# Block 1's fourth pair of heads: three products a chunk, or six DMAs a chunk, in an attention and two-layer MoE kernel

## The chip, the cores and the metric

The kernel runs on one core of a Trainium2 chip. The time is device microseconds of one execution, and less is better. Besides the runs that are timed there is one profiled execution, whose trace is read here.

## The reference

The kernel computes a linear attention with a decaying state and, on its output, two feed-forward layers. Only the state's recurrence and the order of the columns matter here.

```python
# q, k, v, alpha: (4, 8, 768, 48); B, H, S, D
for t in range(S):
    state = alpha[:, :, t, :, None] * state + np.einsum('bhd,bhe->bhde', k[:, :, t], v[:, :, t])
    y[:, :, t] = np.einsum('bhd,bhde->bhe', q[:, :, t], state)
x = y.transpose(0, 2, 1, 3).reshape(B * S, H * D)        # 3072 x 384
x = (x @ w_a) * (x @ w_b) @ w_out                         # d_ff 1536
h = x @ w_in                                              # d_ff 2048
out = (np.maximum(h, 0) + alpha2 * np.minimum(h, 0)) @ w_out2
```

The weights arrive in 64-bit floating point. The kernel converts each on the core to a high and a low 32-bit part, and every large product is made of three (high by high, low by high, high by low).

## The kernel before, in words

**Blocks and chunks.** The 3072 tokens are cut into 24 chunks of 128 (`CH`; one chunk holds 128 time steps of one batch entry), and these into 6 blocks of four chunks (`BC`). Chunk g belongs to block g // 4. Blocks 0 and 1 hold the first 256 steps of all four batch entries. A block's attention output is `x` (`xt[n]`, 128 partitions x high/low x `NJ` = 4 pairs x 512 tokens), and the first layer reads three of the four pairs (`KT` = 3, 384 columns).

**The fourth pair.** The heads have 48 columns and sit in slots of 64 partitions, two to a pair, so four pairs have 16 free partitions in each slot, and the columns of the fourth pair have to fill the free partitions of the first three. That is done in three ways (lines 539 to 677). In block 0 the values are laid out in advance (`vg`) and products place them. In block 1 (`moved`, lines 601 to 617) ScalarE copies the fourth pair's output from PSUM to `shift` (L607), three products with a shifting matrix (L611) add it to the other pairs, and only three pairs are split into high and low (`split_h` L657 on ScalarE, `split_l` L661 on VectorE, two instructions each). In blocks 2 to 5 four pairs are split, and after the block's last chunk six DMAs on SP's queue (L677) copy 16 partitions each from the fourth pair to the others.

**One chunk of attention** (`chunk(g)`, from block 1 on): two scans (L402, L412) and a product with q and k (`mul`, L417) on VectorE; a transpose of k (`kps`, L453) and the scores (`A`, L481) on TensorE; the masked scores (`ev_a`, `As`, L496) on VectorE; `pe_cross` (L558, L581) on TensorE; `mid` (L587) on VectorE; `pe_own` (L558, L565) on TensorE; the next state (`kept`, L632) on VectorE; then the split to `x`. Scores and output of all chunks share one PSUM buffer (`pring`), so a chunk's scores wait until the chunk before has been split.

**The first layer** goes over `SEGMENTS`: block 0 with units 0 and 1, block 1 with units 0 and 1, block 0 with units 2 and 3, and so on; a unit is 256 of the 1536 hidden columns. Each step k of `flat` has nine matmuls `pa`, nine `pb` and, two steps later (`LAG`), nine `acc` (L699, L700, L702). The `pa` and `pb` keep the order of k. Steps 0 to 3 are block 0's with units 0 and 1, step 4 is the first that reads block 1. A unit's weights `wa`, `wb`, `wo` are converted by VectorE and ScalarE (L254 to L283; the last instruction is L283), at most two conversions at a time.

**The order** of every engine's instructions, and of the DMA issues on SP, is fixed at build time by a planner (`Graph.run`). Each operation has an engine, a duration, a latency, a key and what it waits for. The planner steps through its own time and gives an engine that becomes free the ready operation with the lowest key. A user on another engine may begin `HOP` = 250 ns after the end. Where TensorE would be free for over 500 ns, `fill` writes small matmuls that compute nothing (`wp`, L185) for 0.7 of the planned gap, up to block 2. On the chip each engine goes through its fixed order and waits on semaphores.

Of the kernel before, what the change touches and what calls it, by code (L numbers as in the profile page):

```python
# [11 lines left out]
F32 = mybir.dt.float32  # L12
# [9 lines left out]
P = 128  # L22
CH = 128
HC = CH // 2
BC = 4
MB = BC * CH
# [7 lines left out]
ON_PE = (("a", 0), ("b", 0), ("o", 0))  # L34


MM = 228
HOP = 250
T_MOE = 30000
STRETCH = 1.2  # L40
URGENT = 40000
# [8 lines left out]
class Graph:  # L50
# [7 lines left out]
    def add(self, eng, dur, fn, key, deps=(), lat=0, after=(), pool=None):  # L58
        o = Op()
        o.pool, o.hold = pool, []  # L60
        o.eng, o.dur, o.fn, o.key, o.lat = eng, dur, fn, key, lat
        o.users, o.soft, o.ready, o.end, o.need, o.n = [], [], 0, None, 0, len(self.ops)
        for d in {x for x in deps if x is not None}:
            d.users.append(o)
            o.need += 1
        for d in {x for x in after if x is not None}:
            d.soft.append(o)
            o.need += 1
        self.ops.append(o)
        return o  # L70
# [69 lines left out]
def body(tc, akq, v, vg, w_a, w_b, w_o1, w_in, w_o2, beta, out):  # L140
    nc = tc.nc
    NG, H = akq.shape[0], v.shape[2]
    KT, NT = out.shape[1], out.shape[2]
# [3 lines left out]
    NJ = H // 2  # L147
    D = KT * P // H
    GR = 64 - D
    NA = NJ * (CH + 1) + 1  # L150
    NC = NJ * CH
    NB = NG // BC

    with ExitStack() as ctx:
# [3 lines left out]
        xpool, cpool, gpool, tp = pool("xpool", 2), pool("cpool", 2), pool("gpool", 2), pool("tp", 2)  # L158
# [4 lines left out]
        eye = gpool.tile([P, P], F32, name="eye", tag="a_sb")  # L163
# [14 lines left out]
        def fill(t0, t1):  # L178
# [14 lines left out]
            out=mask, in_=mask, pattern=[[1, P]], compare_op=ALU.is_ge, fill=0.0,  # L193
# [2 lines left out]
        nc.scalar.copy(plus, eye)  # L196
        nc.scalar.mul(minus, eye, -1.0)


        shift = gpool.tile([P, KT + 1, P], F32, name="shift", tag="x2")  # L200
        nc.gpsimd.memset(shift, 0.0)
        for t in range(KT):
            for i in range(2):
                nc.gpsimd.tensor_copy(
                    out=shift[:, t, 64 * i + D : 64 * i + 64],
                    in_=eye[:, 64 * i + GR * t : 64 * i + GR * (t + 1)],
                )

        G = Graph(fill)
        units, uses = {}, {}  # L210
# [2 lines left out]
        flat = [(n, i, s) for s, (n, u0, u1) in enumerate(SEGMENTS) for i in range(2 * u0, 2 * u1)]  # L213
        at = [T_MOE + int(k * 27 * MM * STRETCH) for k in range(len(flat) + LAG + 1)]
        due, block_at = {}, {}
# [111 lines left out]
        for u in range(NU1):  # L327
            for nm, src in (("a", w_a), ("b", w_b), ("o", w_o1)):
                x = nm, u
# [16 lines left out]
        st = [dict() for _ in range(NG)]  # L346
        xt, xuse, xdone = {}, {}, {n: [] for n in range(NB)}
        xring, lring, rring, vring, zring = Ring(2), Ring(2), Ring(2), Ring(2), Ring(1)
        aring, pring, kring, sring, yring = Ring(1), Ring(1), Ring(1), Ring(1), Ring(1)
        before = {"scan": None}  # L350
        accfree = [[] for _ in range(KT)]
        state = [[] for _ in range(BC)]
# [1 line left out]
        def chunk(g):  # L354
            s = st[g]
            n, c = divmod(g, BC)
            start, moved, end = n == 0, n == 1, n == NB - 1
            key = block_at[n] - (BC - c) * 9500 - 6000 if n else c * 1000 - 100000
            cols = slice(c * CH, (c + 1) * CH)

            def A(eng, dur, fn, deps, early=0, lat=0, after=()):
                return G.add(eng, dur, fn, key - early, deps, lat, after)
# [3 lines left out]
            if spare is None:  # L366
                rwait, lwait = rring.take(), lring.take()
                rhold, lhold = rring.last(), lring.last()
            else:
                rwait, lwait, rhold, lhold = (), (), [], []  # L370
# [27 lines left out]
            lv = A("SP", 1250 if start else 720, load_v, vring.take(), 12000, 3000)  # L398
# [23 lines left out]
            slack = SLACK if not start else 0  # L422
            k1 = q1 = A("DVE", 1220, mul, [lq, sa], 0, slack)
# [3 lines left out]
            zs = None  # L427
            if not start:
# [5 lines left out]
                zs = A("DVE", 360, decayed, [r, *state[c]])  # L434
# [14 lines left out]
            if not (start and end):  # L449
# [9 lines left out]
                kbank, w, hold = bank(0)  # L459
                x = A("PE", 480, pe_k, [k1, *w])  # L460
# [23 lines left out]
            def ev_a(i):  # L484
                def f():
                    if i == 0:
                        s["At"] = tp.tile([P, 2 * NJ * CH], F32, name="As", tag="As", bufs=1)
                        w = CH if start else HC
                        s["As"] = s["At"][:, 0 : 2 * NJ * w].rearrange("p (i j t) -> p i j t", i=2, j=NJ)
                    if start:  # L490
                        m = mask.rearrange("p (o t) -> p o t", o=1).to_broadcast([P, NJ, CH])
                        nc.vector.tensor_tensor(out=s["As"][:, i], in0=s["A"][i], in1=m, op=ALU.mult)
                        return
                    m = mask[:, 0:HC].rearrange("p (a o t) -> p a o t", a=1, o=1).to_broadcast([P, 2, NJ, HC])
                    a = s["A"].rearrange("p i (j t) -> p i j t", t=HC)
                    nc.vector.tensor_tensor(out=s["As"], in0=a, in1=m, op=ALU.mult)  # L496
                return f

            w = sring.take()
            if start:  # L500
                (b0, w0, h0), (b1, w1, h1) = bank(1), bank(2)
                abanks = (b0, b1)
                pa = A("PE", 1200, pe_a, [k1, q1, *w0, *w1])
                a0 = A("DVE", 660, ev_a(0), [pa, *w])
                a1 = A("DVE", 660, ev_a(1), [pa, a0])
                masked.append(a1)
                h0.append(a0)
                h1.append(a1)
            else:
                pa = A("PE", 600, pe_a, [k1, q1, *pring.take()])  # L510
                a0 = a1 = A("DVE", 700, ev_a(0), [pa, halved[0], *w], 0, slack)
                pring.use(a0)

            def slot_of_head(j, i):
# [2 lines left out]
            def y_of(k, rows=slice(0, P), t=slice(0, CH)):  # L517
                return s["y"][rows, k // 2, k % 2, t]
# [4 lines left out]
            if start:  # L523
# [7 lines left out]
                w = aring.take()  # L531
# [16 lines left out]
                            nc.tensor.matmul(y_of(k, half(p)), s["vg"][:, k, p, :],  # L548
                                             s["As"][:, KT // 2, 2 * (KT % 2) + p, :], start=False, stop=k > 0)

                py = A("PE", 1600, pe_y, [a0, a1, lv, q1, *pring.take()])
                yhold = pring.last()
            else:
                part_of = lambda h: slice(h * HC, (h + 1) * HC)
# [43 lines left out]
                pc = A("PE", 850, pe_cross, [a0, ks, lv, *pring.take()])  # L598
                yhold = pring.last()
                kring.use(pc)  # L600
                z1 = A("DVE", 360, mid, [pc, zs])
                py = A("PE", 850, pe_own, [z1, zs, q1])
                yhold.append(z1)
            if moved:
                def ev_3():
                    s["y3"] = shift[:, KT, :]
                    nc.scalar.copy(s["y3"], y_of(KT))  # L607

                def pe_m():
                    for k in range(KT):  # L610
                        nc.tensor.matmul(y_of(k), shift[:, k, :], s["y3"], start=False, stop=k > 0,  # L611
                                         skip_group_check=True)

                lhold.append(py)
                x = A("ACT", 280, ev_3, [py, *yring.take()])
                py = A("PE", 750, pe_m, [x])
                yring.use(py)
            lhold.extend((pa, py))
            if spare is not None:
                for k, ops in ((spare, rhold), (spare + 1, lhold)):  # L620
# [5 lines left out]
            if not end:  # L626
# [7 lines left out]
                x = A("ACT" if start else "DVE", 360, kept, [ds] if start else [z1, py])  # L634
# [5 lines left out]

            nt = KT if start or moved else NJ
            sring.use(py)
            vring.use(py)

# [16 lines left out]
            if c == 0:  # L663
                xring.take()
                xuse[n] = xring.last()
            s["xh"] = A("ACT", 620, split_h, [py], after=[st[n * BC]["xh"]] if c else ())
            xl = A("DVE", 700, split_l, [s["xh"]])
            yhold.append(xl)
            xdone[n].append(xl)
            if c < BC - 1 or start or moved:  # L670
                return
            moves = []
            for t in range(KT):
                for i in range(2):
                    def move(t=t, i=i):
                        z = xt[n].bitcast(F32)
                        nc.sync.dma_start(z[64 * i + D : 64 * i + 64, :, t, :],  # L677
                                          z[64 * i + GR * t : 64 * i + GR * (t + 1), :, KT, :])

                    moves.append(A("SP", 600, move, xdone[n], 0, 2500))  # L680
            xdone[n] = moves

        masked, halved = [], []
        for g in range(NG):
# [19 lines left out]
        def up(key, deps, x, w, o, after=()):  # L704
# [9 lines left out]

            op = G.add("PE", 9 * MM, f, key, deps, after=after, pool=mpool)
            uses[w].append(op)
# [97 lines left out]
        for k, (n, i, s) in enumerate(flat):  # L814
            u, o = divmod(i, 2)
            x = lambda n=n: xt[n]
            b = {}
            pa, ma, ba = up(at[k], [done["a", u][o], *xdone[n]], x, ("a", u), o,
                            [up_before])
# [30 lines left out]
        for k in range(2 * NU2):  # L850
            b = {}
            key = t0 + k * (t1 - t0) // (2 * NU2)
            _, c = conv((w_in, w_o2)[k % 2][k // 2], f"s{k % 2}", f"s{k % 2}", key,
                        [stored[k - 2]] if k >= 2 else part_users[k], lambda r, b=b: b.update(r=r))
# [10 lines left out]
        for k in range(2 * NU2):  # L865
            x = "id"[k % 2], k // 2
# [54 lines left out]
        for k, (n, i) in enumerate(flat2):  # L921
            if i == 0:
                ld = load_x2(n)
            u, o = divmod(i, 2)
# [97 lines left out]
```

## Time and profile before

| | |
|---|---|
| time, median of 3 runs | 967.0 us (966.63 to 967.01) |
| profiled execution, its own time | 966.85 us |
| span of its instructions | 965.2 us |
| mean granted clock of TensorE | 0.999 |
| busy: PE, VectorE, ScalarE, GpSimd | 952.7, 600.4, 253.9, 4.4 us |

Times in rows count from the first instruction. A timeline row has the start, the duration, the engine, the line, what is written and read, and how many instructions it merges; in brackets stands how long the engine had been idle, and what ended that. Matmuls of a row overlap the next row's, so a step's cost is the distance from its start to the next start.

### The profile page before, as it was taken

The numbers are of one execution on the slowest core, as the hardware profiler recorded it, in microseconds if no ns is written. First come the engines' busy times: TensorE is split into PE (matmuls) and PEld (weight loads), VectorE is DVE, ScalarE is ACT, GpSimd is POOL, SyncE is SP. The second block draws the span as 40 slices with busy tenths as digits, with TensorE's granted clock in tenths as the row PEclk, the third lists the DMA queues.
The fourth block names the chain that finished last, engine by engine and source line by source line (L and its number), as shares of the span: only waits on it lengthen the run. The fifth ranks groups of instructions, "written<-read, shape, count | busy, mean of one in ns | idle before, by whom it ended". The sixth has DMA issues, their size and how long they took to land.

```text
span 965.2 us, 15549 instructions
## 1 busy us (share of the span) xinstructions
PE 952.7 (99%) x6667; PEld 770.4 (80%) x6667; DVE 600.4 (62%) x887; ACT 253.9 (26%) x422; POOL 4.4 (0%) x18
## 2 busy tenths in 40 slices
PE   6999999999999999999999999999999999999998
PEld 5778888778877887887788888888888888888886
DVE  7999888578668868865332254555555545545554
ACT  2444443233333333332221211111111111111111
POOL 1000000000000000000000000000000000000000
PEclk9999999999999999999999999999999999999999
DMA  8971000145456545742065550010100200200000
GB/s 317 407 287 51 12 1 12 45 145 180 150 179 204 206 167 191 240 153 79 25 210 197 196 196 1 27 72 1 65 33 1 89 10 0 99 1 1 33 1 33
DMA packets 31076, 104.09 MB, mean 108 GB/s; under 512 B 3488, under 2 KB 4256, under 8 KB 31008
## 3 DMA queue, kind: packets, MB, share of 16 engines
q1 hardware_dynamic: 30864, 102.97, 30.2%
q8 instruction: 52, 0.85, 0.4%
q10 hardware_dynamic: 144, 0.13, 0.0%
q14 instruction: 16, 0.13, 0.0%
HBM read 74.78 MB, written 26.74 MB: 105 GB/s over the span
## 4 chain that ended last, share of the span: by engine, by line
PE 99%; DVE 0%; DMA 0%; ACT 0%; issue 0%; DVEq 0%; ACTq 0%
PE acc L699 12%; PE acc L702 12%; PE acc L700 12%; PE pi L699 7%; PE pi L702 7%; PE pi L700 7%; PE pb L699 5%; PE pa L699 5%; PE pa L700 5%; PE pb L700 5%; PE pb L702 5%; PE pa L702 5%; PE wp L185 2%; PE y L558 2%; PE kps L453 1%; PE A L481 1%
## 5 line engine op out<-in xcount | busy, mean ns | idle before, releaser
L722 ACT CAST gh<-ng 128x512 fp32r<-128x512 f32 x96 | 59.6, 621 | 328.6 <-DVE ng L935 275.0
L931 DVE TENSOR_SCALAR ng<-pi,betaT 128x512 f32<-128x512 f32 x96 | 72.1, 751 | 106.7 <-PE pi L702 105.8
L726 DVE TENSOR_TENSOR gl<-ng,gh 128x512 fp32r<-128x512 f32 x96 | 66.3, 691 | 79.9 <-ACT gh L722 79.9
L699 PE MATMUL pi<-x,v 128*128 128x512 f32 x288 | 113.3, 393 | 0.0
L700 PE MATMUL acc<-gh,v 128*128 128x512 f32 x288 | 113.1, 393 | 0.0
L702 PE MATMUL acc<-gl,v 128*128 128x512 f32 x288 | 112.9, 392 | 0.0
L700 PE MATMUL pi<-x,v 128*128 128x512 f32 x288 | 112.7, 391 | 0.0
L699 PE MATMUL acc<-gh,v 128*128 128x512 f32 x288 | 112.1, 389 | 0.0
L829 DVE TENSOR_TENSOR a_sb<-a_sb,pb 128x512 f32<-128x512 f32 x72 | 49.4, 686 | 96.5 <-PE pb L702 96.4
L699 PE MATMUL pa<-x,wa 128*128 128x512 f32 x216 | 86.7, 401 | 0.0
L699 PE MATMUL pb<-x,wb 128*128 128x512 f32 x216 | 86.6, 401 | 0.0
L699 PE MATMUL acc<-gh,wo 128*128 128x512 f32 x216 | 86.6, 401 | 0.0
L702 PE MATMUL acc<-gl,wo 128*128 128x512 f32 x216 | 84.9, 393 | 0.0
L700 PE MATMUL pa<-x,wa 128*128 128x512 f32 x216 | 84.7, 392 | 0.0
L700 PE MATMUL pb<-x,wb 128*128 128x512 f32 x216 | 84.6, 392 | 0.0
L700 PE MATMUL acc<-gh,wo 128*128 128x512 f32 x216 | 84.6, 392 | 0.0
L826 ACT COPY a_sb<-pa 128x512 f32<-128x512 f32 x72 | 42.2, 587 | 151.0 <-PE pa L702 151.0
L702 PE MATMUL pi<-x,v 128*128 128x512 f32 x288 | 81.5, 391 | 0.0
L722 ACT CAST gh<-a_sb 128x512 fp32r<-128x512 f32 x72 | 44.8, 622 | 102.6 <-DVE a_sb L829 102.6
L935 DVE SCALAR_TENSOR_TENSOR ng<-pi,ng 128x512 f32<-128x512 f32 x96 | 66.4, 691 | 3.1
L699 PEld LDWEIGHTS pi<-x,v 128*128 128x128 f32 x288 | 54.1, 188 | 13.7 <-DVE ng L935 2.1
L699 PEld LDWEIGHTS acc<-gh,v 128*128 128x128 f32 x288 | 54.0, 188 | 12.3
(120 smaller groups left out, 1426.5 us busy)
## 6 DMA issues: line engine op xcount, KB each, us to landing
kq<-in_akq SPq DMA_DIRECT2D x24, 512.0 KB, 3.8
w2d<-ws SPq DMA_DIRECT2D x16, 768.0 KB, 3.5
v<-w2d SPq DMA_DIRECT2D x16, 768.0 KB, 5.4
x2d<-x SPq DMA_DIRECT2D x18, 512.0 KB, 3.3
x<-x2d SPq DMA_DIRECT2D x6, 1536.0 KB, 6.9
ra<-in_akq SPq DMA_DIRECT2D x24, 258.5 KB, 3.5
v<-in_v SPq DMA_DIRECT2D x24, 256.0 KB, 4.4
rs<-in_w_in SPq DMA_DIRECT2D x8, 768.0 KB, 5.5
```

What stands on the lines that cost most here:

```text
L185: nc.tensor.matmul(wp, warm[:, 0:P], warm, start=True, stop=True)
L453: nc.tensor.transpose(s["kps"][:, j, :], kT()[:, j, :], ident)
L558: nc.tensor.matmul(y_of(k, half(p), part_of(h)), s["v"][part_of(h), 2 * j + i, :], s["As"][part_of(h), i, j, :], start=first, stop=False, ...
L699: nc.tensor.matmul(o, lh, rh, start=first and n == 0, stop=False)
L700: nc.tensor.matmul(o, ll, rh, start=False, stop=False)
L702: nc.tensor.matmul(o, lh, rl, start=False, stop=last and n == len(pairs) - 1)
L722: nc.scalar.copy(gq[idx][0], src())
L726: nc.vector.tensor_tensor(out=gl, in0=src(), in1=gh.bitcast(F32), op=ALU.subtract)
L826: nc.scalar.copy(b["a"], ba["t"])
L829: nc.vector.tensor_tensor(out=b["a"], in0=b["a"], in1=bb["t"], op=ALU.mult)
L931: nc.vector.tensor_scalar(out=b["n"], in0=bh["t"], scalar1=0.0, scalar2=betaT[:, i : i + 1], op0=ALU.min, op1=ALU.mult)
L935: nc.vector.scalar_tensor_tensor(out=b["n"], in0=bh["t"], scalar=0.0, in1=b["n"], op0=ALU.max, op1=ALU.add)
```

## The change

In block 1 all four pairs are split, as in blocks 2 to 5, in one instruction on either engine. After each of its chunks six DMAs copy that chunk's 128 columns (before, six per block copy 512 columns). The copy L607, the products L611 and the table `shift`, which GpSimd built, go. In block 1 the masked scores, `mid` and both splits have a key lower by 100000, which puts them ahead of any conversion that is ready. From block 2 on a chunk's key is lower than before by 10500 to 18000. In the plan a matmul takes 230 ns and not 228; of each VectorE and ScalarE duration 80 and 90 ns are turned into latency, during which the engine is free; and the scores and outputs of block 0's chunks have shorter durations.

```diff
-MM = 228
+MM = 230
+LEAD = {"DVE": 80, "ACT": 90}
...
-        o.eng, o.dur, o.fn, o.key, o.lat = eng, dur, fn, key, lat
+        o.eng, o.dur, o.fn, o.key, o.lat = eng, dur - LEAD.get(eng, 0), fn, key, lat + LEAD.get(eng, 0)
...
-        shift = gpool.tile([P, KT + 1, P], F32, name="shift", tag="x2")
-        nc.gpsimd.memset(shift, 0.0)
-        for t in range(KT):
-            for i in range(2):
-                nc.gpsimd.tensor_copy(
...
-            start, moved, end = n == 0, n == 1, n == NB - 1
-            key = block_at[n] - (BC - c) * 9500 - 6000 if n else c * 1000 - 100000
+            start, end = n == 0, n == NB - 1
+            key = c * 1000 - 100000 if start else block_at[n] - (BC - c) * 12000 - 14000
+            if n == 1:
+                key = block_at[n] - (BC - c) * 9500 - 6000
+            first = 100000 if n == 1 else 0
...
-                pa = A("PE", 1200, pe_a, [k1, q1, *w0, *w1])
+                pa = A("PE", 1120, pe_a, [k1, q1, *w0, *w1])
...
-                a0 = a1 = A("DVE", 700, ev_a(0), [pa, halved[0], *w], 0, slack)
+                a0 = a1 = A("DVE", 700, ev_a(0), [pa, halved[0], *w], first, slack)
...
-                py = A("PE", 1600, pe_y, [a0, a1, lv, q1, *pring.take()])
+                py = A("PE", 1480, pe_y, [a0, a1, lv, q1, *pring.take()])
...
-                z1 = A("DVE", 360, mid, [pc, zs])
+                z1 = A("DVE", 360, mid, [pc, zs], first)
...
-            if moved:
-                def ev_3():
-                    s["y3"] = shift[:, KT, :]
-                    nc.scalar.copy(s["y3"], y_of(KT))
-
-                def pe_m():
-                    for k in range(KT):
-                        nc.tensor.matmul(y_of(k), shift[:, k, :], s["y3"], start=False, stop=k > 0,
-                                         skip_group_check=True)
-
-                lhold.append(py)
-                x = A("ACT", 280, ev_3, [py, *yring.take()])
-                py = A("PE", 750, pe_m, [x])
-                yring.use(py)
...
-            nt = KT if start or moved else NJ
+            nt = KT if start else NJ
...
-            s["xh"] = A("ACT", 620, split_h, [py], after=[st[n * BC]["xh"]] if c else ())
-            xl = A("DVE", 700, split_l, [s["xh"]])
+            s["xh"] = A("ACT", 620, split_h, [py], first, after=[st[n * BC]["xh"]] if c else ())
+            xl = A("DVE", 700, split_l, [s["xh"]], first)
...
-            if c < BC - 1 or start or moved:
+            if start or (n > 1 and c < BC - 1):
                 return
+            xs = cols if n == 1 else slice(0, MB)
...
-                        nc.sync.dma_start(z[64 * i + D : 64 * i + 64, :, t, :],
-                                          z[64 * i + GR * t : 64 * i + GR * (t + 1), :, KT, :])
-
-                    moves.append(A("SP", 600, move, xdone[n], 0, 2500))
-            xdone[n] = moves
+                        nc.sync.dma_start(z[64 * i + D : 64 * i + 64, :, t, xs],
+                                          z[64 * i + GR * t : 64 * i + GR * (t + 1), :, KT, xs])
+
+                    moves.append(A("SP", 600, move, [xl] if n == 1 else xdone[n], 0, 2500))
+            xdone[n] = moves if n > 1 else [x for x in xdone[n] if x is not xl] + moves
```

## Rows read from the trace of the kernel before

**Rows 1.** The page: busy time of each engine, share of the span, instructions.

```profile
PE 952.7 (99%) x6667; PEld 770.4 (80%) x6667; DVE 600.4 (62%) x887; ACT 253.9 (26%) x422; POOL 4.4 (0%) x18
```

**Rows 2.** Waits of PE, whole span: us in total, times, longest.

```profile
PE kps L453 <- DVE kq L417: 8.0, 1, 8.0
```

**Rows 3.** Stretches of PE: length, busy (instructions), granted clock, DMA share, GB/s.

```profile
71.44:89.21 17.77, 17.77 (x220) 1.00 0.28 86
89.21:958.70 869.49, 869.38 (x5607) 1.00 0.26 89
```

**Rows 4.** Groups of PE by line: busy us, mean ns, idle before.

```profile
L185 PE MATMUL wp<-ones 128*128 128x256 bf16 x125 | 17.1, 287 | 0.0
...
L611 PE MATMUL y<-shift 128*128 128x128 f32 x24 | 3.4, 279 | 0.0
```

**Rows 5.** Timeline of PE, 70 to 90 us.

```profile
70.32 1.36 PE L185 MATMUL wp<-ones 128*128 128x256 bf16 x11
71.44 0.47 PE L699 MATMUL pb<-x,wb 128*128 128x512 f32 x1
...
75.65 0.60 PE L453 MATMUL kps<-plus,kq 128*128 128x128 f32 x4
...
76.80 0.50 PE L699 MATMUL pb<-x,wb 128*128 128x512 f32 x1
...
78.98 0.39 PE L699 MATMUL acc<-gh,wo 128*128 128x512 f32 x1
...
81.13 0.46 PE L558 MATMUL y<-As,v 64*64 64x64 f32 x16
...
81.98 0.61 PE L185 MATMUL wp<-ones 128*128 128x256 bf16 x4
82.35 0.48 PE L699 MATMUL acc<-gh,wo 128*128 128x512 f32 x1
...
84.60 0.46 PE L558 MATMUL y<-As,v 64*64 64x64 f32 x16
...
85.44 1.38 PE L185 MATMUL wp<-ones 128*128 128x256 bf16 x11
86.66 0.83 PE L611 MATMUL y<-shift 128*128 128x128 f32 x6
87.33 2.13 PE L185 MATMUL wp<-ones 128*128 128x256 bf16 x18
89.21 0.48 PE L699 MATMUL pa<-x,wa 128*128 128x512 f32 x1
```

**Rows 6.** Timeline of DVE, 69 to 90 us.

```profile
69.69 0.95 DVE L283 TENSOR_TENSOR wb<-c,c 128x768 fp32r<-128x768 f32 x1
...
72.76 1.22 DVE L417 TENSOR_TENSOR kq<-kq,ra 128x1024 f32<-128x1024 f32 x1
73.90 0.68 DVE L829 TENSOR_TENSOR a_sb<-a_sb,pb 128x512 f32<-128x512 f32 x1
...
76.94 0.69 DVE L496 TENSOR_TENSOR As<-A,mask 128x512 f32<-128x512 f32 x1 [0.55 <-PE A L481]
...
88.80 0.61 DVE L661 TENSOR_TENSOR x<-y,x 128x256 fp32r<-128x256 f32 x2
```

**Rows 7.** Timeline of ACT, block 1's last split.

```profile
87.99 0.54 ACT L657 CAST x<-y 128x256 fp32r<-128x256 f32 x2 [0.40 <-DVE Z L632]
```

**Rows 8.** Waits of DVE, 0 to 95 us.

```profile
DVE Z L632 <- ACT x L657: 1.8, 2, 1.3
```

**Rows 9.** Timeline of SP: block 2's six DMAs.

```profile
221.86 4.57 SPq L677 DMA_DIRECT2D x<-x  x6
```

**Rows 10.** Line L677: time from issue to landing of its 24 DMAs.

```profile
DMA to landing us min/median/max: 2.3/2.3/3.3
```

**Rows 11.** Tile x: splits, ns min/median/max; the longest are the four-pair form.

```profile
L657 ACT CAST x<-y x32: 272/478/587, 16.8 to 479.3; 128x512 fp32r<-128x512 f32 x16, 128x256 fp32r<-128x256 f32 x8, 128x128 fp32r<-128x128 f32 x8
L661 DVE TENSOR_TENSOR x<-y,x x32: 277/546/693, 17.4 to 479.9; 128x512 fp32r<-128x512 f32 x16, 128x256 fp32r<-128x256 f32 x8, 128x128 fp32r<-128x128 f32 x8
```

More of the change, by code (lines that the diff above doesn't have):

```diff
@@ L197, in body @@
         nc.scalar.mul(minus, eye, -1.0)
-        shift = gpool.tile([P, KT + 1, P], F32, name="shift", tag="x2")
-        nc.gpsimd.memset(shift, 0.0)
-        for t in range(KT):
-            for i in range(2):
-                nc.gpsimd.tensor_copy(
-                    out=shift[:, t, 64 * i + D : 64 * i + 64],
-                    in_=eye[:, 64 * i + GR * t : 64 * i + GR * (t + 1)],
-                )
         G = Graph(fill)
@@ L348, in body @@
         xring, lring, rring, vring, zring = Ring(2), Ring(2), Ring(2), Ring(2), Ring(1)
-        aring, pring, kring, sring, yring = Ring(1), Ring(1), Ring(1), Ring(1), Ring(1)
+        aring, pring, kring, sring = Ring(1), Ring(1), Ring(1), Ring(1)
         before = {"scan": None}
```

## The prediction

> **What bounds the kernel now.** The first view is the page: TensorE is busy for 99% of the span [rows 1], and it waits for another engine once, 8.0 us at the start [rows 2]. That alone would say that only less TensorE work can help. The groups by line correct it: 17.1 us of the busy time are filling matmuls `wp` that compute nothing [rows 4]. They stand where the plan expected TensorE to have nothing to do, so they are the waits to look for. So I cut the span at the last of them. From 89.21 us, where step 4 begins (the first that reads block 1), TensorE is busy for 869.38 of 869.49 us at full clock [rows 3]: no filler, no wait, a fixed amount of work. Nothing can be gained behind that point as long as the work there is the same; it can only be lost. The time is therefore the moment at which step 4 starts plus a constant, and the question is how far the change moves 89.21.
>
> What holds that moment? I follow it backwards. Step 4 starts 0.4 us after VectorE began block 1's last split at 88.80 (0.61 us long) [rows 5, 6]. That split waited for ScalarE's at 87.99 [rows 7], this for the shifting products at 86.66, these for the last `pe_own` at 84.60, for `pe_cross` at 81.13, for the transpose and the scores at 75.65 to 76.80 and, first of all, for VectorE's product with k and q at 72.76 [rows 5, 6]. VectorE gets to it late because it converts unit 1's weights until then: `wb` is written at 69.69 + 0.95 = 70.64, and TensorE's first `pb` with it is at 71.44.
>
> **The stretch from `pb` at 71.44 to step 4, as a sum** [rows 5]. Blocks of nine matmuls: 71.44 to 75.65 holds two (4.21), 76.80 to 78.98 one (2.18), 78.98 to 81.13 one (2.15), 82.35 to 84.60 one (2.25): 10.79 us. The last chunk's attention: 75.65 to 76.80, 81.13 to 81.98, 84.60 to 85.44: 2.84. The shifting products: 86.66 to 87.33: 0.67. Filler: 81.98 to 82.35, 85.44 to 86.66, 87.33 to 89.21: 3.47. Together 17.77, which is the length of the stretch [rows 3].
>
> **The change, part by part.**
>
> *The products go.* 24 matmuls of L611 have 3.4 us of busy time [rows 4]; the last group takes 0.67 us from start to start, so four groups take about 2.7 us of TensorE. Only the last group lies on the path directly. The other three lie where TensorE also runs filler. What they give is time for VectorE: `kept` (L632) may no longer wait behind product and split, where VectorE stood idle for 1.8 us in two waits, the longest 1.3 [rows 8]. I take the longer one, 1.3 us, as saved before `wb` is done (bounds 0 and 1.8). Four copies on ScalarE and the table's building on GpSimd go too; neither engine is near its limit (26% and 0% [rows 1]), so I cost them at nothing, and without that slack the copies would be worth some 0.3 us each.
>
> *Four pairs are split instead of three.* The longest form takes 0.59 us on ScalarE and 0.69 on VectorE [rows 11], against 0.54 and 0.61 [rows 6, 7]: 0.08 us more on VectorE a chunk, 0.3 for four. VectorE is the busy engine there, so this counts against the 1.3.
>
> *Filler.* `wb` is ready at 70.64 and `pb` starts at 71.44, because eleven filling matmuls stand in front [rows 5, 6]. The plan took VectorE for slower than it is: the product at 72.76 lasts 1.22 us, but the next instruction starts after 1.14 [rows 6], and that 0.08 is what the change takes off every duration of VectorE. With a truer plan I expect half of the 0.8 us back (bounds 0 and 0.8). So `pb` starts at 71.44 - 1.3 + 0.3 - 0.4 = about 70.0.
>
> *The DMAs come in.* Behind the last `pe_own` now stand ScalarE's split (0.59), VectorE's (0.69), a hand-over of about 0.1 us each, and six issues on SP. Block 2's six issues started over 4.57 us [rows 9], so I take 0.64 us from one to the next, five steps or 3.2 us, up to 3.8 at the view's mean of 0.76. The last lands 2.3 us after its issue, 3.3 at most [rows 10]. Tail: 0.7 + 0.8 + 3.2 + 2.3 = 7.0 us; upper end 8.6; lower end 6.4, if the first three of step 4's nine matmuls need only the earlier DMAs. Before, the same distance was 85.44 to 89.21, or 3.8 us. The tail is thus 3.2 us longer than what it replaces. The other chunks' 18 DMAs have ten microseconds and more before step 4; SP has to wait for each split before it issues them, and the loads queued behind were due far ahead, so they cost nothing unless a load turns out late. DMA is at a share of 0.28 in this stretch [rows 3].
>
> The row shows 2.3 us for 64 KB. The Trainium skill (DMA: Bandwidth & Descriptors, section on the anatomy of one DMA) speaks against cutting a transfer in four: a fixed part of about 2.0 us that size doesn't touch, plus bytes over 436 GB/s, given for DMAs that GpSimd issues. By it a 16 KB piece would land in an estimated 2.04 us, and the forecast below would be 0.3 us lower; no row here shows a piece of that size.
>
> *First on their engines.* What the tail costs depends on how many blocks of nine matmuls TensorE still has when the last `pe_own` ends. Before, `pe_cross` came after `acc` of step 2 and `pe_own` after that of step 3, so none was left. The masked scores and `mid` now go ahead of everything on VectorE, and every chunk is shorter by a copy, a product and their hand-overs, so the shared PSUM buffer is free sooner. I expect two of the five blocks (4.3 us) to move behind `pe_own`.
>
> *Other keys and durations.* From block 2 on attention goes earlier. With TensorE at 869.38 of 869.49 us [rows 3] there is nothing to win; reordering costs at worst some short waits, bounds 0 and 2 us, and I take 0.
>
> **Sum.** Step 4 at 70.0 + 10.8 + 2.84 + (7.0 - 4.3) = 86.3, that is 2.9 us earlier. The profiled execution's 966.85 becomes 963.95; the median of the runs stands 0.15 above it, so 964.1 us.
>
> **The rivals**, by the blocks left to cover the tail (0.2%, or 1.9 us, is about what a measurement of this kernel can tell from no change):
>
> 1. *All is hidden.* VectorE finds a gap for the last chunk's product between the conversions, so attention runs before `wb` is ready and the tail lies under the five blocks. Step 4 at 70.0 + 13.6 = 83.6 or, with both upper bounds for VectorE, 82.8: 967.0 - 5.6 = 961.4 us, or 960.6. For it: the chain through the shared buffer is shortened four times, by 0.67 us of products and a copy each. Against: unit 1's conversions keep the lower keys, and they fill VectorE to 72.76. Chance 0.3.
> 2. *One block is left, a trade.* The product's time turns into waiting for DMAs: exposed 7.0 - 2.15 = 4.85, step 4 at 88.5, 966.3 us. For it: in the trace before both orders were decided against attention. Chance 0.22.
> 3. *Slower: the order stays, and the DMAs stand alone.* Place: behind `pe_own` of block 1's last chunk. With no block left the whole tail is exposed: 70.0 + 13.6 + 7.0 = 90.6, or 968.4 us; with the tail's upper end 8.6 it is 970.0. It decides from about 1.4 us of cover downwards (step 4 then starts later than 89.21), and passes 0.2% once the exposed part is over 7.5. For it: an issue on SP costs 0.64 us six times, and the row of landing is no shorter than the three products were. Against: the four steps are now first. Chance 0.12.
> 4. *The new keys make TensorE wait behind 89.21*, which takes back the forecast's 2.9 us and more: 967 to 970 us. The rows show no slack there, but none is needed so far either. Chance 0.06.
>
> **How the numbers follow.** The forecast, two blocks left, has 0.3 and its own range, from the bounds of the terms, is 962.6 (0.9 for `pb` at its upper gains, 0.6 for the tail's lower end) to 967.4 (1.7 for `pb` without any, 1.6 for the tail's upper end). The 80% range takes in the hidden case, with 1.6 us below 960.6 for fillers further ahead that may go too, and the slower rival up to its middle: 959.0 to 969.2. Faster by over 0.2% (below 965.1): the hidden case, most of the forecast and a fifth of the trade: 0.58. Within 0.2%: the rest of the trade and the forecast, and part of rivals 3 and 4: 0.30. Slower (above 968.9): 0.12.
>
> **What the profile after would show.** No L611 and L607; 24 more issues at L677; filler below 17.1 us; `pb` of step 2 before 71.44; after the last `pe_own` of block 1 two blocks of nine matmuls and then filler or a wait of some 2.7 us; step 4 at about 86.3; behind it TensorE without gaps for the same 869.5 us up to its last blocks of `acc`. It would be wrong if step 4 starts at 88 us or later, if the last `pe_own` is still the last work before step 4, or if TensorE waits anywhere behind step 4.

## The result and the profile after

The changed kernel takes 958.62 us (median of 4 runs, 958.04 to 959.31) against 967.0: a ratio of 0.9914 (95% interval 0.9896 to 0.9931). I had forecast 964.1 with a range of 959.0 to 969.2. The direction was right; the gain of 8.4 us was almost three times the 2.9 I gave, and lies just outside the range.

The profiled execution took 958.35 us, 8.5 less than that of before. The page's row of engines, changed kernel, and the two waits of TensorE that its view of waits has:

```profile
PE 944.7 (99%) x6589; PEld 763.2 (80%) x6589; DVE 600.8 (63%) x883; ACT 253.1 (26%) x414; POOL 2.2 (0%) x11
```

```profile
PE kps L448 <- DVE kq L412: 7.8, 1, 7.8
PE A L476 <- DVE x L642: 0.5, 1, 0.5
```

TensorE's share is 99% as before [rows 1]; what fell is its amount, by 8.0 us. One wait of 0.5 us is new [rows 2]; it is at 35.5 us, ahead of step 4. Stretches of the changed kernel (length, then per engine busy time and instructions, clock, DMA share, GB/s):

```profile
36.15:69.03 32.88, 32.88 (x548) 24.66 (x542) 32.73 (x52) 15.26 (x26) 0.00 (x0) 1.00 0.74 271
69.03:81.44 12.41, 12.41 (x109) 9.87 (x103) 12.38 (x21) 6.38 (x10) 0.00 (x0) 1.00 0.68 246
81.44:951.00 869.56, 869.51 (x5606) 704.71 (x5604) 523.35 (x760) 218.48 (x350) 0.00 (x0) 1.00 0.26 91
```

Step 4 starts at 81.44 and not at 89.21: 7.8 us of the 8.5. Behind it TensorE is as full as before [rows 3]; from step 4 to the start of the last matmul it is 871.2 us in both. The rest is at the end: from that start to the end of the span 4.0 us instead of 4.8.

The timeline of TensorE before step 4, changed kernel:

```profile
62.58 0.46 PE L553 MATMUL y<-As,v 64*64 64x64 f32 x16
...
65.62 0.60 PE L448 MATMUL kps<-plus,kq 128*128 128x128 f32 x4
66.15 0.70 PE L476 MATMUL A<-kq 48*64 48x64 f32 x32
66.78 1.48 PE L186 MATMUL wp<-ones 128*128 128x256 bf16 x12
68.19 0.46 PE L553 MATMUL y<-As,v 64*64 64x64 f32 x16
...
69.03 0.50 PE L681 MATMUL pb<-x,wb 128*128 128x512 f32 x1
...
71.31 0.46 PE L553 MATMUL y<-As,v 64*64 64x64 f32 x16
...
72.15 0.51 PE L681 MATMUL pa<-x,wa 128*128 128x512 f32 x1
...
74.35 0.39 PE L681 MATMUL pb<-x,wb 128*128 128x512 f32 x1
...
76.41 0.39 PE L681 MATMUL acc<-gh,wo 128*128 128x512 f32 x1
...
78.47 1.05 PE L186 MATMUL wp<-ones 128*128 128x256 bf16 x8
79.28 0.48 PE L681 MATMUL acc<-gh,wo 128*128 128x512 f32 x1
...
81.44 0.39 PE L681 MATMUL pa<-x,wa 128*128 128x512 f32 x1
```

Compare [rows 5]: the last chunk's scores and `pe_cross` are now ahead of `pb` (66.15, 68.19), and its `pe_own` (71.31) stands behind one of the five blocks, not behind all. Four blocks are left to cover the DMAs, so filler falls to 0.81 us (78.47 to 79.28) from 3.47. VectorE, changed kernel:

```profile
62.62 1.22 DVE L412 TENSOR_TENSOR kq<-kq,ra 128x1024 f32<-128x1024 f32 x1
...
64.63 0.68 DVE L642 TENSOR_TENSOR x<-y,x 128x512 fp32r<-128x512 f32 x1
...
66.91 0.69 DVE L491 TENSOR_TENSOR As<-A,mask 128x512 f32<-128x512 f32 x1
67.52 0.95 DVE L275 TENSOR_TENSOR wb<-c,c 128x768 fp32r<-128x768 f32 x1
...
73.83 0.68 DVE L642 TENSOR_TENSOR x<-y,x 128x512 fp32r<-128x512 f32 x1
```

The last chunk's product with k and q is at 62.62 and no longer at 72.76 [rows 6], ahead of `wb`. The third chunk's last split is at 64.63 (before: 71.37). The last chunk's own split is at 73.83, and the six DMAs follow on SP, the last of them at 77.73:

```profile
74.54 3.78 SPq L659 DMA_DIRECT2D x<-x  x6
```

From the line's view, for these six and for all 24 of block 1:

```profile
DMA to landing us min/median/max: 1.9/3.0/4.1
...
DMA to landing us min/median/max: 1.8/2.6/4.1
```

Of the six the first takes 4.1 us and the last 1.9, so the last lands at 79.6. That is 1.8 us before step 4: in the changed kernel the DMAs are covered, and something else sets step 4.

Filler is down from 17.1 us in 125 matmuls [rows 4] to 10.2 in 71 (length, PE, PEld; `wp` alone):

```profile
0.00:36.15 36.15, 7.17 (x48) 5.06 (x48) 1.00 0.93 345
36.15:81.44 45.29, 3.04 (x23) 1.99 (x23) 1.00 0.73 264
```

### The profile page after: what moved, and what is told of

Read it like the earlier page. It is cut to its first block, busy times and chain, and to the rows that moved or that the text cites. A ratio compares the mean times of both kernels' runs of the same rounds, so it can differ in the third digit from the quotient of the medians.

```text
span 956.6 us, 15389 instructions
## 1 busy us (share of the span) xinstructions
PE 944.7 (99%) x6589; PEld 763.2 (80%) x6589; DVE 600.8 (63%) x883; ACT 253.1 (26%) x414; POOL 2.2 (0%) x11
## 4 chain that ended last, share of the span: by engine, by line
PE 97%; DVE 2%; issue 0%; DMA 0%; ACT 0%; DVEq 0%; ACTq 0%
PE acc L681 12%; PE acc L684 12%; PE acc L682 12%; PE pi L681 7%; PE pi L682 7%; PE pi L684 7%; PE pa L681 6%; PE pb L681 5%; PE pa L682 5%; PE pb L684 5%; PE pa L684 5%; PE pb L682 5%; PE y L553 2%; PE A L476 1%; PE kps L448 1%; PE y L576 1%
```

## The experiments

Theory A: the durations in the plan decide the order, and the order is the gain. Theory B: the gain is the removal of the products. Theory C: being first on their engines covers the tail. Theory D: what counts is when the last chunk's chain starts. The runs are told in groups; one table at the end has the instants. A ratio is to runs of the kernel before that were taken beside the run (their medians are 966.2 to 966.9 us).

**1. DMAs alone.** The new move of the fourth pair, all numbers and keys of the kernel before (edit of the changed kernel, in part):

```diff
-LEAD = {"DVE": 80, "ACT": 90}
+LEAD = {}
...
-            first = 100000 if n == 1 else 0
+            first = 0
```

and `MM`, block 0's durations and the later keys as before. 

> Only the DMAs replace the products; durations, keys and order rules of the kernel before. Theory A (the durations in the plan made the gain: they put the last chunk's product with k and q ahead of unit 1's wb): without them that product stays behind wb, at about 72 us, the DMA tail of 7.0 us is exposed, step 4 starts at 89 us or later, 967 to 970 us. Theory B (the gain is the products' removal: 2.7 us of TensorE, and a shorter chain from chunk to chunk): product at about 63 us as in the changed kernel, step 4 at about 82, 958 to 960 us.

Measured: 975.99 us, 1.0097 of before (1.0080 to 1.0114). Theory B falls, and the change's headline edit alone is a loss. The tail stands uncovered, as in my slower rival:

```profile
84.75 6.94 PE L186 MATMUL wp<-ones 128*128 128x256 bf16 x62
91.44 0.47 PE L681 MATMUL pa<-x,wa 128*128 128x512 f32 x1
```

From the end of `pe_own` (84.75) to step 4 it is 6.7 us, and step 4 comes 2.2 us later than before. The other 7 us are lost behind step 4, at the start of block 3, which no theory had (last section).

**2. Durations alone**, on the kernel before:

```diff
+LEAD = {"DVE": 80, "ACT": 90}
...
-        o.eng, o.dur, o.fn, o.key, o.lat = eng, dur, fn, key, lat
+        o.eng, o.dur, o.fn, o.key, o.lat = eng, dur - LEAD.get(eng, 0), fn, key, lat + LEAD.get(eng, 0)
```

> Only the 80 and 90 ns of the VectorE and ScalarE durations become latency; products, keys and TensorE durations of the kernel before. Theory A: the last chunk's product with k and q goes ahead of wb or close to it, step 4 at 83 to 86 us, 961 to 964 us. Theory B: no change, 966 to 968 us.

Measured: 966.36 us, ratio 1.0000 (0.9991 to 1.0010). Theory A alone falls too. The product moved up to 69.54, yet the last chunk's masked scores came later than before (81.01 against 76.94), and so did the third chunk's split (76.67 against 71.37).

**3. All but the DMAs**: the lines with `shift`, `ev_3` and `pe_m` stay, the rest is changed. 

> All of the change but the DMAs: products and the copy to shift stay in block 1, three pairs are split. Theory A: like the changed kernel but for the products' 2.7 us of TensorE, so 960 to 962 us. Theory B: the gain is gone, 965 to 968 us.

Measured: 964.05 us, ratio 0.9979 (0.9969 to 0.9990). That lies between the two theories: beside the other edits the products cost 5.4 us more than the DMAs do (by the medians; 6.3 by the ratios), at least twice their 2.7 us of TensorE, and the rest without the DMAs still gains a little.

**4. All but first:**

```diff
-            first = 100000 if n == 1 else 0
+            first = 0
```

> All of the change, but block 1's masked scores, mid and splits keep their chunk's key. Theory A or B alone: within 1 us of the changed kernel, 958 to 960 us. Theory C (being first on their engines is what gets the tail covered): the last split comes some 5 us later, behind conversions, TensorE has no block left to cover the DMAs, step 4 at 86 to 88 us, 963 to 966 us.

Measured: 964.30 us, 0.9978 (0.9969 to 0.9987), as theory C had it but for one block that is left: the last split is at 80.56, TensorE has one block behind `pe_own` and then 4.87 us of filler, and step 4 is at 86.58. So neither the DMAs nor the durations gain by themselves, and without being first most of the gain is gone. Being first alone was not run.

**5 and 6. The start of the last chain.** In the changed kernel the product is held back; in the kernel before it is pulled forward:

```diff
-            k1 = q1 = A("DVE", 1220, mul, [lq, sa], 0, slack)
+            k1 = q1 = A("DVE", 1220, mul, [lq, sa, *(done["b", 1] if g == 2 * BC - 1 else ())], 0, slack)
...
+            soon = 20000 if g == 2 * BC - 1 else 0
...
-            k1 = q1 = A("DVE", 1220, mul, [lq, sa], 0, slack)
+            k1 = q1 = A("DVE", 1220, mul, [lq, sa], soon, slack)
```

(in the second also for the two scans and the reciprocal). 

> The changed kernel, but the product with k and q of block 1's last chunk also waits until unit 1's wb is converted, so it moves from 62.6 to about 68.5 us. Theory D (what counts is that the last chunk's chain starts ahead of wb, because then TensorE's five blocks cover the DMAs): the product-to-step-4 distance stays at 17 to 19 us, step 4 at 86 to 88, 962.5 to 965.5 us. Rival (TensorE's own work sets step 4 at 81.4 and the chain has slack): within 1.5 us of the changed kernel, 958 to 960 us.

> The kernel before, but scans and product of block 1's last chunk have a key lower by 20000 and go ahead of unit 1's conversions (product at 63 to 66 us instead of 72.8). Theory D: step 4 at 81 to 84 us, 959 to 962 us, with products and without any DMA. Theory B' (the products keep each chunk of block 1 in the shared PSUM buffer longer, and VectorE's sum of work is the same, so an earlier product alone only delays the weights): step 4 at 88 to 91, 965.5 to 968.5 us.

Held back: 965.21 us, 0.9989 (0.9979 to 0.9998); product at 69.56, step 4 at 86.72, as theory D said. Pulled forward: 969.90 us, 1.0030 (1.0018 to 1.0042), slower than either expectation, so theory D is only half the cause. The view of VectorE of that run points at the other half:

```profile
63.57 1.22 DVE L418 TENSOR_TENSOR kq<-kq,ra 128x1024 f32<-128x1024 f32 x1
...
74.33 0.61 DVE L662 TENSOR_TENSOR x<-y,x 128x256 fp32r<-128x256 f32 x2
78.56 0.68 DVE L497 TENSOR_TENSOR As<-A,mask 128x512 f32<-128x512 f32 x1
```

The product is done at 65 us, but the scores wait until the third chunk has left the shared PSUM buffer, at 75. The scans and the product that now go first put this split off by 3.0 us, and the weights as well (`wb` from 69.69 to 73.21), so this run alone doesn't tell the buffer from the weights. The run with the product held back shows what early weights alone are worth. Its TensorE:

```profile
68.06 0.48 PE L681 MATMUL pb<-x,wb 128*128 128x512 f32 x1
...
82.42 4.54 PE L186 MATMUL wp<-ones 128*128 128x256 bf16 x40
86.72 0.48 PE L681 MATMUL pa<-x,wa 128*128 128x512 f32 x1
```

The first `pb` with unit 1's weights is 1.0 us earlier than in the changed kernel (69.03), and step 4 is 5.3 us later, behind filler. In runs 3, 4 and 7 `pb` is early too (68.23, 66.47, 67.12) and step 4 late. So early weights alone do not bring step 4 forward.

**7. All but the durations of VectorE and ScalarE** (`LEAD = {}`). 

> All of the change, but no part of a VectorE or ScalarE duration becomes latency. Theory A (the durations decide the order): the last chunk's product goes back behind the conversions, 71 us or later, the tail has no cover, step 4 at 90 to 93 us, 967 to 971 us. Theory B: 958 to 961 us.

Measured: 968.47 us, 1.0016 (1.0006 to 1.0025). Here the buffer is free early enough (split at 69.54), but the product is at 75.95: the tail has no cover, step 4 at 90.11.

**8. All but the later keys:**

```diff
-            key = c * 1000 - 100000 if start else block_at[n] - (BC - c) * 12000 - 14000
+            key = c * 1000 - 100000 if start else block_at[n] - (BC - c) * 9500 - 6000
```

> All of the change, but from block 2 on the chunks have the keys of the kernel before. If the new keys are needed: step 4 stays at 81.4, but TensorE waits at a start of block 2 to 5, as the run with DMAs alone did for 4.4 us at 318 to 325 us, so 960 to 966 us. If they are not: no wait behind step 4, 958 to 959.5 us.

Measured: 958.13 us, 0.9912 (0.9897 to 0.9926), the changed kernel's time. They neither gain nor guard anything with this order.

**9. Once per block**: block 1's DMAs copy 512 columns after its last chunk (`xs = slice(0, MB)`, and the return of blocks 2 to 5). 

> The changed kernel, but block 1's six DMAs copy 512 columns once, after its last chunk, as in blocks 2 to 5. Theory D (only the last chunk's tail counts, and it has the same six issues either way): last landing within 1 us of the changed kernel's, 957.5 to 959.5 us. Rival (the pieces matter, because a larger DMA lands later or SP's queue is free sooner): more than 1 us off to either side.

Measured: 959.18 us, 0.9923 (0.9908 to 0.9937), 0.6 us from the changed kernel and with overlapping runs (958.79 to 960.43). The last DMA lands at 79.9 there (77.4 and 2.5 us to landing), 0.3 us after the changed kernel's, as theory D said. Cutting the transfer by chunk costs and gives nothing that these runs can tell.

**10 and 12. TensorE's durations**: all of them as before (`MM = 228`, 1200, 1600), then block 0's alone. 

> All of the change, but TensorE's planned durations are those of before (228, 1200, 1600 ns). If only the VectorE and ScalarE durations matter: 957.5 to 960 us, step 4 at 81 to 83. If the order hangs on every number of the plan: a different order around unit 1's conversions, product or last split 3 us or more later, step 4 at 84 to 88, 961 to 966 us.

> All of the change, but block 0's scores and outputs have their old planned durations (1200 and 1600 ns); a matmul stays at 230. Theory E (step 4 follows the later of two things, the last chunk's product with k and q and the third chunk's last split, by about 17 us): with both at 62 to 65 us as in the changed kernel 958 to 960 us; with either at 69 us as in the run with all old TensorE durations, step 4 at 85 to 87 us, 963 to 968 us, and then the 2 ns a matmul are not what that run lost.

Measured: 968.41 us, 1.0017 (1.0008 to 1.0026), and 960.81 us, 0.9938 (0.9921 to 0.9954). With all of them old, the product is at 61.05 but the third chunk's split at 69.06, step 4 at 85.97, and TensorE waits again at the start of block 2, for 3.2 us and at a granted clock of 0.64 (225 to 232 us), which puts the time above both expectations. With block 0's alone step 4 is at 83.59, between the two values that the expectation named. The two runs differ in nothing but the 2 ns a matmul: step 4 comes 2.4 us later with them gone, and the time is 7.6 us longer. A number of the plan works through the order of instructions and the filler alone.

**11. No filler** (`fill` is never called). 

> The changed kernel without the filling matmuls; the order is otherwise the same. If the fillers stand in front of ready work: about 0.5 us at 68 us and 1 to 2 us in the first 35 us come back, 956 to 958.5 us. If they only fill waits and keep TensorE at its higher clock: TensorE's waits appear where the fillers were (9 us), the granted clock is below 1.0 in the first 90 us, 958.5 to 963 us.

Measured: 959.26 us, 0.9932 (0.9914 to 0.9950), runs from 957.52 to 962.34. Step 4 is at 80.68, 0.8 us sooner, and the granted clock is 1.00 in the first 82 us. The time lies in the second expectation's range, but the lower clock that it named did not come. So fillers stand in front of little that is ready, and in these stretches the clock doesn't need them; whether leaving them out gains anything is not told by runs that far apart.

**The instants** (us, from the profiled executions; the last column is the median time):

| run | product, last chunk | split, third chunk | masked scores, last chunk | step 4 | time |
|---|---|---|---|---|---|
| before | 72.76 | 71.37 | 76.94 | 89.21 | 967.0 |
| changed | 62.62 | 64.63 | 66.91 | 81.44 | 958.6 |
| 1 DMAs alone | 74.96 | 71.32 | 79.57 | 91.44 | 976.0 |
| 2 durations alone | 69.54 | 76.67 | 81.01 | 89.00 | 966.4 |
| 3 all but DMAs | 68.08 | 72.29 | 74.76 | 86.17 | 964.1 |
| 4 all but first | 66.57 | 70.65 | 73.58 | 86.58 | 964.3 |
| 5 product held | 69.56 | 65.02 | 74.37 | 86.72 | 965.2 |
| 6 product early | 63.57 | 74.33 | 78.56 | 90.83 | 969.9 |
| 7 old durations | 75.95 | 69.54 | 79.68 | 90.11 | 968.5 |
| 8 old late keys | 62.20 | 64.20 | 66.48 | 81.01 | 958.1 |
| 9 once per block | 62.85 | 64.86 | 67.14 | 82.53 | 959.2 |
| 10 old TensorE durations | 61.05 | 69.06 | 71.40 | 85.97 | 968.4 |
| 11 no filler | 62.40 | 64.41 | 66.62 | 80.68 | 959.3 |
| 12 old block 0 durations | 62.22 | 66.84 | 68.78 | 83.59 | 960.8 |

The masked scores start 1.9 to 4.8 us after the later of the two columns ahead of them, in every row. Most edits move both columns. Run 5 moves the product alone (by 6.9 us, the split by 0.4), and step 4 comes 5.3 us later than in the changed kernel. Runs 12 and 10 come nearest to moving the split alone: the product is no later than in the changed kernel, the split 2.2 and 4.4 us later, and step 4 2.2 and 4.5. No run moves the split by an edit of its own.

Step 4 follows the masked scores by 8.0 to 15.4 us, so not by a fixed distance. In the changed kernel five blocks, `pe_own` and 0.8 us of filler fill the time from `pb` to step 4, and `pb` starts right behind `pe_cross`, 0.6 us after `wb` is written. Whether the scores or the weights hold it there was not tried.

## Why the prediction was right and wrong

- *The bound* was read rightly: the time is the instant of step 4 plus a constant. From step 4 to the end of the span it is 875.2 us in the changed kernel, 876.0 before, and 875 to 878 in all runs but 1, 10 and, in its profiled execution, 12.
- *The step that failed* is the overlap, under "First on their engines": I left the last chunk's whole attention behind `pb` and expected two blocks of cover for the DMAs. Four blocks moved behind `pe_own`, and scores and `pe_cross` went ahead of `pb`. The sum's terms against the changed kernel: `pb` at 70.0, measured 69.03; five blocks 10.8, measured 10.76; attention behind `pb` 2.84, measured 0.84; exposed tail 2.7, measured none, but 0.81 of filler, where `acc` of step 3 waits for VectorE (without filler TensorE waits 0.5 us there, run 11). That is 86.34 against 81.44: of the 4.9 us between them 2.0 are attention, 1.9 the tail and 1.0 `pb`.
- *The head of the chain* is why the overlap came out wrong. I followed the last releaser and named VectorE's product at 72.76 alone, late because VectorE "converts unit 1's weights until then". But `wb` is written at 70.64, and more stands between (VectorE, kernel before):

```profile
71.37 0.61 DVE L661 TENSOR_TENSOR x<-y,x 128x256 fp32r<-128x256 f32 x2
71.90 0.95 DVE L283 TENSOR_TENSOR wo<-c,c 128x768 fp32r<-128x768 f32 x1
```

The first is the third chunk's split, which through the shared PSUM buffer holds the same scores. It ends at 71.98, the product at 73.98. The prediction gives the shared buffer as a reason, but has no instant and no term for it. The change moved both up: the split to 64.63, the product to 62.62. In runs 3 and 4 (with the products, without being first) both are later than in the changed kernel and the split is the later one; in run 7 (old durations) both are later and the product is the later one.
- *Rival 1*, all hidden, to which I gave 0.3, is what happened, with its condition, a gap for the product between the conversions. Its sum still kept the 2.84 of attention behind `pb`, although its words put attention ahead of the weights; so even it was late, by 2.2 us (83.6) or 1.4 (82.8).
- *The tail* of 7.0 us was well sized: 6.7 us in run 1, where nothing covers it. In the changed kernel the six issues take 3.78 us as estimated. A 16 KB piece lands sooner than the 64 KB ones (2.3 us at the least [rows 10]) where little else is moving. The last six of run 1, at a DMA share of 0.33:

```profile
DMA to landing us min/median/max: 1.8/1.8/2.0
```

In the changed kernel, at a share of 0.69, they take 1.9 to 4.1. The Trainium skill (DMA: Bandwidth & Descriptors, on the anatomy of one DMA) gave an estimated 2.04 for such a piece; run 1 comes near it, the changed kernel's slower pieces don't, and the measurement decides.
- *The products at 2.7 us of TensorE* was right as a cost and wrong as a price: with all the rest changed they are worth 5.4 us against the DMAs (run 3).
- *Filler, durations*: I priced the truer plan at 0.4 us of filler. It is worth nothing alone (run 2) and 9.8 us together with the rest (run 7 against the changed kernel). I had no term for parts that only gain together.
- *Later keys*: 0, as forecast (run 8). *The slower rival* is what the DMAs do alone (run 1), and 6 us more, behind step 4.

## What to carry to other kernels

When two chains reach the same wait within a microsecond or two, follow both back. Pulling one forward gained nothing here where the other came later (runs 2 and 6), and a sum over single edits misses that all of them together gain. A kernel whose order is planned from estimated durations should be read as one with an order to choose; small numbers in the plan move several us, so look at where the late instruction stands and not at the cost of the edit. A long transfer may replace a short product if the work that covers it is put there by the same change; by itself it was a loss here (run 1).

## What was not expected of the hardware

A short wait late in the kernel can cost more than itself. In run 1 TensorE waited four times at the start of block 3, for 4.4 us in all (timeline of TensorE):

```profile
318.50 0.69 PE L476 MATMUL A<-kq 48*64 48x64 f32 x32 [1.20 <-DVE x L642]
321.00 0.71 PE L553 MATMUL y<-As,v 64*64 64x64 f32 x16 [1.80 <-DVE As L491]
...
323.00 1.12 PE L448 MATMUL kps<-plus,kq 128*128 128x128 f32 x4 [0.47 <-DVE kq L412]
325.08 0.76 PE L681 MATMUL pa<-x,wa 128*128 128x512 f32 x1 [0.96 <-DMA x<-x]
...
326.06 0.63 PE L681 MATMUL pa<-x,wa 128*128 128x512 f32 x1
326.49 0.63 PE L682 MATMUL pa<-x,wa 128*128 128x512 f32 x1
...
329.05 0.63 PE L681 MATMUL pb<-x,wb 128*128 128x512 f32 x1
...
329.85 0.39 PE L681 MATMUL pb<-x,wb 128*128 128x512 f32 x1
330.07 0.39 PE L682 MATMUL pb<-x,wb 128*128 128x512 f32 x1
```

and by stretches (length, PE, granted clock, DMA share, GB/s):

```profile
318.00:325.00 7.00, 3.35 (x84) 0.61 0.80 272
325.00:329.00 4.00, 3.92 (x9) 0.50 0.91 229
...
333.00:340.00 7.00, 7.00 (x32) 1.00 0.40 129
```

After the waits the clock is at 0.50, its 1.2 GHz level, and a matmul takes 0.43 us from start to start instead of 0.23. From step 4 to the last matmul's start run 1 needs 8.0 us more than before, of which 4.4 are waits. The nine `pa` from 325.08 to 329.05 account for 1.9 of the rest: 3.97 us, where the changed kernel's nine `pb` at 74.35 take 2.06. Not every wait does this: in run 11 waits of up to 1.4 us between 12 and 82 us left the granted clock at 1.00.

One wait of 1.92 us at the start of block 2 was followed by a clock of 0.59 over 4.2 us in the profiled execution of run 12 (963.93 us, its other runs 959.76 to 961.10). There VectorE, and ScalarE with it, stood behind a load of weights that had not landed:

```profile
222.41 0.56 DVE L249 TENSOR_SCALAR c<-rs 128x768 uint32<-128x768 uint32 x1 [2.20 <-DMA rs<-in_w_in]
```

In run 1 VectorE waits for no load there; why the waits arise in runs 1 and 10 and not in the others was not tried.
